# Last section of a long convolution on one Trainium2 core: inverse transform with exchanged operands, blocks turned on TensorE, additions on VectorE and GpSimd, and a new ranking of the convolution's steps

## The chip, the cores and the metric

The kernel runs on one core of one Trainium2 chip. In this text PE is TensorE, DVE is VectorE, ACT is ScalarE, POOL is GpSimd and SP the queue that starts DMA transfers. PSUM is the memory that TensorE writes. The metric is the device time of one execution in microseconds, as the median of the runs shown; smaller is better.

## What is computed

One sequence of 2,048 tokens with 512 channels goes through a state-space convolution and then through a shifting MLP, each behind a layer norm and each with a residual.

```python
def _A_ref(u, ...):                       # u: 1 x 2048 x 512, after a layer norm
    dt = jnp.exp(log_dt)
    A = -jnp.exp(log_A_real) + 1j * A_imag          # 512 x 128
    C = (C_real + 1j * C_imag) * dt[:, None]
    P = jnp.exp((A * dt[:, None])[:, :, None] * pos[None, None, :])
    K = 2.0 * jnp.einsum("dn,dnl->dl", C, P).real   # 2048 taps per channel
    y = irfft(rfft(u, 2L) * rfft(K, 2L))[..., :L]
    return y + u * D_skip
def _B_ref(x, w1, w2, w3, w4):
    h = gelu(layernorm(x) @ w1)
    hs = concat(h shifted by +1, -1, +2, -2 tokens, a quarter of the channels each) @ w2
    x1 = x + hs
    return x1 + gelu(layernorm(x1) @ w3) @ w4       # 512 -> 1792 -> 512
h  = x + _A_ref(layernorm(x), ...)
h2 = h + _B_ref(layernorm(h), ...)
```

## The kernel before, in words

**Two phases.** `conv_phase` computes the first of the last two lines, `mixer_phase` the second. The array `h` (128 partitions x 16 x 512 channels) holds the sequence in fp32: token groups q = 0 to 3 are four slices of four. The mixer starts with group 3: its normalised values are turned by PE (tiles xt), split into a high and a low part (xt30h, xt30l and so on: cast on ACT, difference on DVE), and multiplied by w1 (tiles l).

**The convolution as matmuls.** Channels are worked in four sections s of 128. The transform of length 4,096 is factored into 32 by 64 points, so each transform is two stages of small matmuls with tables: `fas` and `tbs` forward, `ms` and `fis` back. For each of eight frequency groups e, `product` (919) makes the second forward stage (matmuls of at with tbs) and multiplies spectrum and taps on DVE, or on POOL where a table says so; the results lie in u, thp, ini. `stage_b_inv` (974) then does the first inverse stage: `ms` is the stationary operand (64 x 128), the products move (128 columns), and an eviction ("ibv") writes 512 columns into at, in the order channel, k, pair. `turn_inv` (996) turns a quarter of a section with one stream transpose on DVE, in blocks of 32 by 32. `stage_a_inv` (1001) does the last inverse stage with `fis` and adds h, either with an identity matmul into the same bank and a copy by ACT, or with an addition on DVE.

**The last section.** Its last stage is `last_a_inv` (1024): four stream transposes; four identity matmuls that bring h into four banks; 64 matmuls with fis of 128 columns each, group 3 first; the statistics of group 3 straight from PSUM (DVE bn_stats); and four copies by ACT into h. After it come nodes for the norm of group 3 (1236 to 1240). The mixer's `norm1(3)` (1332) scales group 3 on DVE into the tile xq0, in a pool of its own (1253), and `turn1` (1344) has PE turn it into the four tiles xt3_0 to xt3_3. Two of these lie in the memory of banks 2 and 3 of the convolution.

**What sets the order.** In the convolution nothing is written in the order in which it runs. Each step is a node of `Plan` (153) with an engine, a cost, what it reads and writes, and a need for PSUM banks. `order` (194) fills each engine's queue step by step: among the steps that could start within 0.05 us of the first, the one with the lowest number in the table `RANK` is taken. A second table, `SHARE` (23), says which evictions go to DVE, which sums and products go to POOL, and where `pads` (759) puts two fillers. A filler (`busy`, 774) is an identity matmul of 128 columns whose result nobody reads; `order` adds more of them where its model of PE has a gap. The mixer's steps are issued in the order of the code. All instructions but a few are recorded at one line, 140, that of the helper that passes them on; names of tiles tell them apart.

## Time and profile before

| what | value |
|---|---|
| median of 3 runs | 677.06 us (676.99 to 678.91) |
| profiled execution | 676.15 us |
| its span | 673.9 us |
| its mean granted TensorE clock | 0.992 |
| PE busy | 641.1 us |
| DVE busy | 575.4 us |
| ACT busy | 403.9 us |
| POOL busy | 398.8 us |

The span runs from the first to the last instruction of the profiled execution, and 2.25 us of its time lie outside. Times in the timeline are from the span's start. A row of the timeline has the start, the length, engine, line, operation, destination and sources, and in brackets the idle time ahead of it with what ended it. An fp32 matmul leaves two records, a transpose on PE one, so "x16" of matmuls are eight of them. The chain of waits is followed back from the last instruction: each row is a stretch of the chain on one engine. The granted clock (PEclk) is shown as a share of full speed. "bank" is a PSUM bank of the convolution.

### The profile page before, as it was taken

What the parts mean: (1) busy time and instruction counts of PE and PEld (TensorE: products, weight loads), DVE (VectorE), ACT (ScalarE), POOL (GpSimd) and SP (SyncE); (2) the same over time, 40 slices, a digit from 0 to 9 for tenths busy, and PEclk for the clock granted to TensorE, in tenths of its full rate; (3) what the DMA queues carried; (4) which work ended last, traced back from release to release, by engine and by line L of the source; (5) the groups of instructions that cost most, each with busy time, mean ns of one, the idle gap of its engine ahead of it and who ended that gap; (6) DMA issues with size and microseconds to landing.
All of it is one profiled execution on the core that took longest, in us unless ns stands there. A gap on an engine that the chain in (4) does not pass through costs nothing.

```text
span 673.9 us, 17729 instructions
## 1 busy us (share of the span) xinstructions
PE 641.1 (95%) x7226; PEld 508.9 (76%) x7226; DVE 575.4 (85%) x991; ACT 403.9 (60%) x700; POOL 398.8 (59%) x411
## 2 busy tenths in 40 slices
PE   2959999999999999999999999999999999999997
PEld 2956657772777585768888888888888889999985
DVE  5999999999899999889978799866688678888896
ACT  7998879888798883246534455544465344435430
POOL 1959799899788798502676219355611644456340
PEclk9989999999899999999999999999999999999999
DMA  8944632000301233020262524455654355434104
GB/s 207 291 132 123 207 120 45 18 3 2 82 3 50 61 102 95 2 63 4 61 202 56 164 79 160 153 184 166 212 190 141 96 169 188 126 112 140 32 0 126
DMA packets 51957, 73.58 MB, mean 109 GB/s; under 512 B 7332, under 2 KB 26788, under 8 KB 51876
## 3 DMA queue, kind: packets, MB, share of 16 engines
q1 hardware_dynamic: 50212, 69.82, 34.0%
q10 hardware_dynamic: 1152, 1.57, 1.0%
q0 software_dynamic: 512, 1.05, 0.7%
q8 instruction: 57, 0.93, 0.6%
q14 instruction: 24, 0.20, 0.1%
HBM read 44.90 MB, written 21.23 MB: 98 GB/s over the span
## 4 chain that ended last, share of the span: by engine, by line
PE 70%; DVE 13%; ACT 7%; issue 3%; POOL 3%; DMA 3%; SPq 1%; DVEq 0%; ACTq 0%; POOLq 0%
PE l L140 20%; PE bank L140 14%; PE acc L140 7%; ACT pt L140 4%; DVE at L140 4%; PE l3e L140 3%; PE l3a L140 3%; PE l3d L140 3%; PE l3g L140 3%; PE l3f L140 3%; PE l3b L140 3%; PE l3c L140 3%; PE res L140 2%; DVE cs L140 2%; DMA h<-in_A_u_dram 2%
## 5 line engine op out<-in xcount | busy, mean ns | idle before, releaser
L140 POOL TENSOR_TENSOR pt<-p,s 128x512 int32<-128x512 int32 x64 | 70.9, 1120 | 6.7 <-DVE sn L140 6.0
L140 ACT ACTIVATE pt<-pt 128x1056 f32<-128x1056 int32 x64 | 69.8, 1097 | 7.6 <-DVE cs L140 4.6
L140 PE MATMUL bank<-at,tbs 128*64 128x128 f32 (+1 forms) x768 | 65.1, 314 | 2.6 <-ACT kt L140 0.9
L140 PEld LDWEIGHTS bank<-at,tbs 128*64 128x64 f32 x768 | 45.3, 135 | 18.7 <-DVE at L140 2.5
L140 PE MATMUL bank<-u,ms 64*128 64x128 f32 x736 | 47.6, 279 | 0.6 <-DVE u L140 0.4
L140 PEld LDWEIGHTS bank<-ident 128*128 128x128 f32 x310 | 37.7, 198 | 13.1 <-issue 5.2
L140 PEld LDWEIGHTS bank<-u,ms 64*128 64x128 f32 x736 | 43.0, 188 | 5.8 <-issue 2.2
L140 DVE TENSOR_TENSOR cs<-pt,amx 128x512 f32<-128x512 f32 x64 | 41.6, 679 | 2.1 <-ACT pt L140 1.5
L140 PE MATMUL bank<-ident 128*128 128x128 f32 x310 | 41.7, 288 | 0.8 <-DVE at L140 0.7
L140 POOL TENSOR_TENSOR cs<-pt,amp 128x512 f32<-128x512 f32 x26 | 32.6, 1255 | 9.4 <-ACT pt L140 5.4
L140 ACT ACTIVATE pt<-pt,halfpi 128x1056 f32<-128x1056 f32 x32 | 38.0, 1186 | 0.1
L140 POOL TENSOR_TENSOR sn<-pt,amp 128x512 f32<-128x512 f32 x28 | 34.0, 1217 | 3.8 <-issue 2.0
L140 ACT COPY at<-bank 128x512 f32<-128x512 f32 x37 | 23.1, 627 | 21.5 <-PE bank L140 21.4
L140 PE MATMUL bank<-cs 128*32 128x64 f32 x1024 | 32.4, 224 | 2.4 <-DVE cs L140 1.3
L140 DVE STREAM_TRANSPOSE at<-bank 128x512 f32<-128x512 f32 (+1 forms) x36 | 33.2, 948 | 1.1 <-PE bank L140 1.0
L140 PEld LDWEIGHTS bank<-cs 128*32 128x32 f32 x1024 | 23.8, 110 | 13.4 <-issue 4.2
L140 PE MATMUL bank<-sn 128*32 128x64 f32 x1024 | 31.9, 221 | 0.3 <-issue 0.2
L140 DVE TENSOR_TENSOR u<-xs,bank 128x1024 f32<-128x1024 f32 x23 | 27.9, 1216 | 3.4 <-ACT xs L140 3.0
L140 PE MATMUL bank<-h,fas 32*32 32x512 f32 x256 | 23.1, 752 | 6.8 <-ACT h L140 5.8
L140 DVE TENSOR_TENSOR amx<-E,amx 128x512 f32<-128x512 f32 (+1 forms) x32 | 26.4, 825 | 3.2 <-ACT amx L140 3.0
L140 POOL TENSOR_TENSOR cs0w<-raw,cs0w 128x512 fp32r<-128x512 f32 x5 | 6.5, 1299 | 36.5 <-ACT cs0w L140 36.3
L140 POOL TENSOR_TENSOR amp<-E,ec 128x512 f32<-128x512 f32 x23 | 24.6, 1074 | 4.1 <-DVE E L140 2.7
(1278 smaller groups left out, 2156.2 us busy)
## 6 DMA issues: line engine op xcount, KB each, us to landing
raw<-in_B_w_dram SPq DMA_DIRECT2D x28, 256.0 KB, 2.9
xq<-xq SPq DMA_DIRECT2D x72, 64.0 KB, 2.0
h<-in_A_u_dram SPq DMA_DIRECT2D x32, 128.0 KB, 4.1
h<-in_A_u_dram SPq DMA_DIRECT2D x16, 256.0 KB, 4.2
kept<-ptw SPq DMA_DIRECT2D x8, 512.0 KB, 4.4
ms<-in_mm_dram SPq DMA_DIRECT2D x4, 768.0 KB, 6.6
ptw<-kept SPq DMA_DIRECT2D x6, 512.0 KB, 6.0
out_dram<-h SPq DMA_DIRECT2D x48, 64.0 KB, 1.7
```

The lines of the kernel that those rows point to most:

```text
L140: ins = f(*args, **kw)
```

## The change

It has four parts.

1. **First inverse stage of the last section** (`PET = (3,)`): the products become the stationary operand and `ms` moves, 128 columns, read so that neighbours are 32 elements apart. The result has channels as partitions, and its eviction writes 512 single elements a partition in an order (x r e a b) that suits a plain 128 by 128 transpose.
2. **Turning on PE**: `turn_pe` transposes four 128 by 128 blocks into a bank, and an eviction of 512 columns ("tev", on ACT but for one on DVE) brings them back to at. The four stream transposes on DVE go.
3. **Last stage** (`last_a_back` in place of `last_a_inv`): 16 matmuls with fis of 512 contiguous columns. Only group 3 gets h by an identity matmul. For groups 0 and 2 DVE adds the bank to h; for group 1 ACT copies the bank to the memory of ms, and POOL adds that to h. The scaling of group 3, four DVE instructions, becomes a step of the plan and writes into the tile `uu`, which the convolution's buffers u0 and u1 are now parts of and which also serves as the mixer's xq0.
4. **Tables**: `RANK` and `SHARE` are new throughout, so the steps of all sections are ordered and shared out anew.

```diff
-SHARE = {'amy': [0, 1, 2, 3, 5, 6, 7, ...
+SHARE = {'tev': [(3, 7)], 'amy': [0, 1, 2, 3, 5, 6, 7, ...
...
+PET = (3,)
+TAIL = ('dve', 'pool', 'dve')
...
-    uu = [tile(f"u{i}", [128, 8 * W]) for i in range(2)]
+    cst["uu"] = tp.tile([128, 16 * W], F32, tag="uu", name="uu")
+    cst["home"] = lambda name: tp.tile([128, 16 * W], F32R, tag="uu", name=name)
+    uu = [cst["uu"][:, i * 8 * W : i * 8 * W + 8 * W] for i in range(2)]
...
+                        if s in PET:
+                            pe.matmul(plan.view(p)[:, par, pair * 128 : pair * 128 + 128], q[f, t, pair, :],
+                                      ms[f, m, e * 2 + pair, :].rearrange("p (h r i) -> p i h r", h=2, r=2),
+                                      start=(i == 0), stop=(i == len(terms) - 1))
+                            continue
                         pe.matmul(plan.view(p)[:, par, pair * w_ : pair * w_ + w_], ms[f, m, e * 2 + pair, :], q[f, t, pair, :],
                                   start=(i == 0), stop=(i == len(terms) - 1))
...
+        if s in PET:
+            dst = at[:, 0].rearrange("p (x e r a b) -> p e a b x r" if len(PET) == NS else "p (x r e a b) -> p e a b x r", e=8, r=2, a=2, b=2)[:, e]
+            src = lambda: plan.view(p)[:, :, 0:256].rearrange("p a (b x r) -> p a b x r", b=2, r=2)
...
+    def turn_pe(s, n, g, gk):
+        def tr():
+            for m in range(4):
+                i = n * 4 + m
+                pe.transpose(plan.view(p)[:, m * 128 : m * 128 + 128], at[:, 0, i * 128 : i * 128 + 128], ident)
+        p = add("PE", 0.43, tr, dense=0.0, r=[("a0", e, n) for e in RE], bank=1, w=gk)
+        evac("tev", (s, n), 512, 0.48, g, lambda: plan.view(p)[:, 0:512], w=gk, frees=p)
...
+    def last_a_back(s):
+        g = at[:, 1].rearrange("p (q i n) -> p q i n", q=4, i=2)
...
+        add("ACT", 1.5, lambda: act.activation(tiny, halfpi, AF.Sqrt), r=[("a1", q, j) for q in quads(s) for j in range(2)])
+        for q in (3, 0, 1, 2):
+            for i in range(2):
+                turn_pe(s, i * 4 + q, g[:, q, i], [("g", q, i), ("a1", q, i)])
+            if q == 3:
+                def keep():
+                    pe.matmul(plan.view(ps[3]), ident, hold(3), start=True, stop=False)
...
+            for i in range(2):
+                def mm(q=q, i=i):
+                    for c in (i, i + 2):
+                        pe.matmul(plan.view(ps[q])[quarter(c)], fis[:, c // 2, :], g[:, q, i], start=q != 3, stop=True)
...
+            if q == 3:
...
+                add("DVE", 0.85, part, r=[("bs", j) for j in range(12, 16)], w=[("hq", q), "part"])
+                add("ACT", 0.5, lambda: act.copy(hold(3), view_(3)), w=[("hq", 3), ("held", 3)], frees=ps[3])
+            elif TAIL[q] == "dve":
+                add("DVE", 0.6, lambda q=q: v.tensor_tensor(hold(q), hold(q), view_(q), ALU.add), r=HK, w=[("hq", q), ("held", q)], frees=ps[q])
+            else:
+                far_ = lambda q=q: ms[:, 0, 0:4, :]
+                add("ACT", 0.5, lambda q=q, far_=far_: act.copy(far_(), view_(q)), w=[("hq", q), ("held", q)], frees=ps[q])
+                add("POOL", 1.35, lambda q=q, far_=far_: gp.tensor_tensor(hold(q), hold(q), far_(), ALU.add), r=HK + [("held", q), "scaled"])
...
-            last_a_inv(s)
+            (last_a_back if s in PET else last_a_inv)(s)
...
+    x3 = cst["x3"] = [cst["uu"][:, i * 512 : i * 512 + 512] for i in range(4)]
+    for i in range(4):
+        add("DVE", 0.46, lambda i=i: v.tensor_scalar(x3[i], h[:, 12 + i, :], cst["mv"][:, 12 + i, 0:1], cst["norm"][2][:, 1, 12 + i : 13 + i], ALU.subtract, ALU.mult),
+            r=["norm", ("held", 3)], w=[("x3", i)] + [("u", i // 2, k) for k in range(2)] + ["scaled"] * (i == 3), port=True)
...
-    XQ = [(w1p if i else w1a).tile([128, 4 * 512], F32, tag=f"xq{i}", name=f"xq{i}") for i in range(4)]
+    XQ = [w1p.tile([128, 4 * 512], F32, tag=f"xq{i}", name=f"xq{i}") if i else cst["uu"] for i in range(4)]
...
     def norm1(q):
+        if q == 3:
+            XL[3] = list(cst["x3"])
+            return
```

In PE's queue the convolution ended before with the last inverse block (ini, ms), two fillers, the identity matmuls of h, and the narrow matmuls with fis, bank by bank:

```order
L140 MATMUL bank0_94<-ini_109,ms_101 128x128 x8
L140 MATMUL bank1_95<-ident_61 128x128
L140 MATMUL bank3_97<-ident_61 128x128
L140 MATMUL bank2_96<-h_66,ident_61 128x512
L140 MATMUL bank3_97<-h_66,ident_61 128x512
L140 MATMUL bank0_94<-h_66,ident_61 128x512
L140 MATMUL bank1_95<-h_66,ident_61 128x512
L140 MATMUL bank0_94<-at_99,fis_103 32x4x32 x16
L140 MATMUL bank2_96<-at_99,fis_103 32x4x32 x8
```

In PE's queue of the changed kernel, the same place has transposes (ident, at) and quads with fis by turns, up to the first transpose xt of the mixer:

```order
L144 MATMUL bank0_94<-ms_101,ini_109 128x128 x8
L144 MATMUL bank2_96<-h_66,ident_61 128x512
L144 MATMUL bank3_97<-ident_61,at_99 128x128 x4
L144 MATMUL bank0_94<-ident_61,at_99 128x128 x4
L144 MATMUL bank1_95<-ident_61,at_99 128x128 x4
L144 MATMUL bank2_96<-at_99,fis_103 32x512 x4
L144 MATMUL bank3_97<-ident_61,at_99 128x128 x4
L144 MATMUL bank0_94<-ident_61,at_99 128x128 x4
L144 MATMUL bank1_95<-ident_61,at_99 128x128 x4
L144 MATMUL bank3_97<-at_99,fis_103 32x512 x4
L144 MATMUL bank0_94<-at_99,fis_103 32x512 x4
L144 MATMUL bank2_96<-ident_61,at_99 128x128 x4
```

One identity matmul of h is left of four, the two fillers are gone, and the matmuls with fis stand in four quads, each behind transposes whose evictions it reads. Behind the last row come four more transposes into bank 3, the last quad into bank 2, and the transposes xt.

ACT's queue at that place in the changed kernel, from the second eviction of transposes to the cast of the mixer (rb from ra is the square root of group 3's norm):

```order
L144 COPY at_99<-bank1_95 128x512
L144 COPY at_99<-bank3_97 128x512
L144 COPY at_99<-bank0_94 128x512
L144 COPY at_99<-bank1_95 128x512
L144 ACTIVATE rb_60<-ra_59 128x2x4
L144 COPY h_66<-bank2_96 128x4x128
L144 COPY ms_101<-bank3_97 128x512
L144 COPY at_99<-bank2_96 128x512
L144 COPY at_99<-bank3_97 128x512
L144 CAST xt30h_4103<-xt3_0_4089 128x512
```

And ACT's queue at the same place before, from the load of the square root's table to the casts:

```order
L140 ACT_TABLE_LOAD
L140 ACTIVATE tiny_72<-halfpi_71 128x1
L140 COPY h_66<-bank0_94 128x4x128
L140 ACTIVATE rb_60<-ra_59 128x2x4
L140 COPY h_66<-bank3_97 128x4x128
L140 COPY h_66<-bank2_96 128x4x128
L140 COPY h_66<-bank1_95 128x4x128
L140 CAST xt30h_4110<-xt3_0_4096 128x512
```

Before, only copies into h stood there, with the square root between the first two; now the square root and two copies that free banks 2 and 3 are queued behind evictions of transposes, and the table is loaded further ahead.

The other place is PE's queue near the 64 narrow matmuls with fas and kt that come ahead of a group of taps (cs). Before:

```order
L140 MATMUL bank1_95<-h_66,fas_102 32x16x16x2 x8
L140 MATMUL bank0_94<-fas_102,kt_118 64x32 x32
L140 MATMUL bank1_95<-ident_61 128x128 x2
L140 MATMUL bank1_95<-fas_102,kt_118 64x32 x32
L140 MATMUL bank2_96<-cs0_124 32x64 x4
```

And in PE's queue of the changed kernel:

```order
L144 MATMUL bank0_94<-h_66,fas_102 32x16x16x2 x8
L144 MATMUL bank1_95<-ident_61 128x128 x2
L144 MATMUL bank1_95<-fas_102,kt_118 64x32 x32
L144 MATMUL bank0_94<-ident_61 128x128 x2
L144 MATMUL bank0_94<-fas_102,kt_118 64x32 x32
L144 MATMUL bank2_96<-cs0_124 32x64 x4
```

Two more fillers stand ahead of the first 32 narrow matmuls, and the two halves have changed places.

More of the change, by code (lines that the diff above doesn't have):

```diff
@@ L125, in tables @@
             mm[f, 2, n, r], mm[f, 2, n, i] = -st, ct
+    if len(PET) == len(WID):
+        fi = fi.reshape(2, 2, 8, 4, 64).transpose(0, 2, 1, 3, 4).reshape(128, 2, 32).copy()
     return {"fa": fa, "fi": fi, "tb": tb, "mm": mm}
@@ new lines, in stage_b_inv, with stage_a_back, mm @@
+        evac("ibv", (s, e), n, 0.22 + n * 0.51e-3, dst, src, w=keys, frees=p)
+    def turn_pe(s, n, g, gk):
[5 more added lines that the diff above has]
+        evac("tev", (s, n), 512, 0.48, g, lambda: plan.view(p)[:, 0:512], w=gk, frees=p)
+    def stage_a_back(s, q):
+        hv = h[:, q * 4 : q * 4 + 4, OFF[s] : OFF[s + 1]]
+        u = uu[q % 2].rearrange("p (i n) -> p i n", i=2)
+        hadd = OFF[s] // 64 + q // 2 in SHARE["hadd"]
+        for i in range(2):
+            turn_pe(s, i * 4 + q, u[:, i], [("u", q % 2, i)])
+        def mm():
+            b = plan.view(p)
+            if hadd:
+                pe.matmul(b, ident, hv, start=True, stop=False)
+            for c in (0, 2, 1, 3):
+                pe.matmul(b[quarter(c)], fis[:, c // 2, :], u[:, c % 2], start=not hadd, stop=True)
+        p = add("PE", 2.24 if hadd else 1.12, mm, dense=0.76, r=[("u", q % 2, i) for i in range(2)] + ["fis", ("h", s, q)], bank=1)
+        if hadd:
+            add("ACT", 0.5, lambda: act.copy(hv, plan.view(p).rearrange("p (j d) -> p j d", j=4)), w=[("h", s, q)], frees=p)
+        else:
+            add("DVE", 0.6, lambda: v.tensor_tensor(hv, hv, plan.view(p).rearrange("p (j d) -> p j d", j=4), ALU.add),
+                w=[("h", s, q)], frees=p)
@@ L1252, in mixer_phase @@
     tm = pool("tm", 6)
[L1253 removed]
+    w1p = pool("wrap", 1)
     sm = pool("sm", 2)
@@ L1758, in mixer_phase @@
             keep3(s + 1)
-    XH = [(w1p if i else w1a).tile([128, 4 * 512], F32R, tag=f"xq{i}", name=f"xh{i}") for i in range(4)]
+    XH = [w1p.tile([128, 4 * 512], F32R, tag=f"xq{i}", name=f"xh{i}") if i else cst["home"]("xh0") for i in range(4)]
     spare = w1p.tile([128, 512], F32R, tag="rawa", name="spare")
```

32 lines of the change are left out of this document (22 added, 10 removed), and 106 rows, old and new, of the table RANK.

## The prediction

> **What bounds the kernel now.** I read the page first: the busy times, and the shares of the chain of waits.
>
> ```profile
> span 673.9 us, 17729 instructions
> PE 641.1 (95%) x7226; PEld 508.9 (76%) x7226; DVE 575.4 (85%) x991; ACT 403.9 (60%) x700; POOL 398.8 (59%) x411
> PE 70%; DVE 13%; ACT 7%; issue 3%; POOL 3%; DMA 3%; SPq 1%; DVEq 0%; ACTq 0%; POOLq 0%
> ```
>
> PE is busy for 95% of the span and carries 70% of the chain. So a change pays where PE waits, or by taking PE time away. The place of this change is the end of the convolution, so I went next to the chain there (start, length, engine, destination).
>
> ```profile
> 267.39 10.98 PE bank L140 x140
> ...
> 285.03 1.18 PE bank L140 x16
> 286.23 0.61 ACT at L140
> 286.87 4.72 DVE at L140 x4
> 291.63 2.82 PE bank L140 x60
> 294.47 1.14 ACT h L140 x2
> 295.65 1.47 PE xt L140 x10
> 297.22 0.59 ACT xt30h L140
> 297.86 8.75 PE l L140 x36
> ```
>
> Until 286.2 the chain is PE alone. Then it changes engines seven times before the mixer's products (l) begin at 297.86: an eviction, four stream transposes on VectorE, the last stage of the inverse on PE, copies to h, the transposes xt, the cast. The timeline has the same stretch with what each waited for.
>
> ```profile
> 286.67 3.60 PE L140 MATMUL bank<-h,ident 128*128 128x512 f32 x8
> 286.85 1.28 ACT L140 ACT_TABLE_LOAD   x1
> 291.63 3.92 PE L140 MATMUL bank<-at,fis 128*32 128x128 f32 x104 [0.17 <-DVE at L140]
> 292.18 0.89 DVE L140 BATCH_NORM_STATS2 bs<-bank 128x6 f32<-128x128 f32 x4 [0.60 <-PE bank L140]
> 293.71 0.21 ACT L140 ACTIVATE rb<-ra 128x8 f32<-128x8 f32 x1
> 294.80 1.93 DVE L140 TENSOR_SCALAR xq<-h,mvh,rr 128x512 f32<-128x512 f32 x4
> 300.63 0.19 PEld L140 LDWEIGHTS l<-xt33l,cs0w 128*128 128x128 f32 x1 [0.34 <-DVE xt33l L140]
> ```
>
> From the last inverse product (286.2) to l (297.86) lie 11.6 us, in which PE does useful work but never all the time. The last row is PE's last wait in the first group of l: it loses 0.34 to VectorE's xt33l, so what reaches the end is what this point moves by.
>
> **The tail, step by step.** The four transposes on VectorE (4.72) and the 64 narrow matmuls go. In their place come 32 transposes on PE, eight evictions of 512 columns, and 16 matmuls of 512 columns; three of four matmuls that carry h through PSUM go (0.90 each, from the 3.60), and two additions on VectorE and one on GpSimd take their work. Prices come from these rows:
>
> ```profile
> 267.24 0.68 DVE L140 TENSOR_TENSOR h<-h,bank 128x512 f32<-128x512 f32 x1
> 267.39 1.29 PE L140 MATMUL bank<-u,fis 128*32 128x512 f32 x8
> 284.85 0.69 DVE L140 COPY at<-bank 128x512 f32<-128x512 f32 x1
> 306.44 1.91 PE L140 MATMUL xt<-ident,xq 128*128 128x128 f32 x16
> ```
>
> Four transposes cost 0.48 (a quarter of 1.91), an eviction 0.6 on ScalarE and 0.69 on VectorE, an addition out of PSUM 0.68. Four matmuls of 512 columns into the four column groups are one quad. Before, a quad reads pairs of elements and takes 1.29; a plain 512-column matmul takes 0.90. The new quads read contiguous columns, so each lies between 0.90 and 1.29, and I expect the lower half.
>
> Walk from 286.2. The eviction ends at 286.9. PE transposes group 3 and the first half of the next until 288.4; the evictions are done by 288.7; the quad of group 3 ends near 289.9, and the statistics start about 290.05, 2.1 earlier than 292.18. The square root now stands behind five evictions on ScalarE and runs near 292.0, while its input would be ready at 291.5. So the four scalings start 1.8 earlier than 294.80, at 293.0, and end at 295.0. If that were what decides, 1.8 would be won.
>
> It isn't, I think. Groups 1, 0 and 2 still go through PE, ScalarE and PE again. ScalarE's evictions end near 292.4 (six of 0.6 with PE's gaps between). Then come in its queue the square root 0.21, the copy of group 3 (0.6) that frees the bank for the last group's first four transposes, and the copy of group 1 (0.6) that frees the bank for its second four. These end near 294.4; eviction 0.6 and a hand-over take it to 295.0; the last quad ends between 295.7 and 296.5. VectorE's addition (0.69) gives 296.5 to 297.2. The first xt transpose writes the memory that this bank held, so it waits for that addition. Ten transposes at 0.12 are 1.2: 297.7 to 298.4, then the cast 0.59 and l at 298.4 to 299.1, 0.6 to 1.3 later than 297.86. Part of this is absorbed by the wait of 0.34 on xt33l, so 0.4 to 1.1 remain. With quads in their lower half I take **+0.5**. GpSimd's addition for group 1 and the load of the square root's table (1.28, now under matmuls) delay nothing: nobody but the later normalisation reads that part of h.
>
> **The operand exchange.** Eight blocks (one for each e) of 64 records swap stationary and moving operand. The nearest rows are these:
>
> ```profile
> 277.25 1.10 PE L140 MATMUL bank<-at,tbs 128*64 128x128 f32 x16
> ...
> 285.03 1.16 PE L140 MATMUL bank<-ini,ms 64*128 64x128 f32 x16 [0.23 <-DVE ini L140]
> ```
>
> Today's block streams contiguous columns in 1.16; the block before it reads pairs, 8 bytes at a time, in 1.10. Pairs cost nothing over contiguous reading. After the change each block streams ms element by element, 128 bytes apart, which no row of this kernel does. By both rows the price is zero and no gain is in it, for records and columns stay the same. The upper bound is the only ratio in the trace that reading could explain, the quad's 1.29 over 0.90, 1.43 times: 0.50 a block, 4.0 in all, in full on the chain, since PE is unbroken from 267.39. I take zero, the nearer rows. [...]
>
> The evictions of these blocks write single elements too. They keep their length of 512 columns, and lie beside PE's work, except the last, which is in the walk.
>
> **The new ranking.** The order of PE's groups before the tail is nearly unchanged. What I could price is one place, after the taps' small matmuls (columns of the windows: PE, PEld, DVE, ACT, POOL busy, PEclk).
>
> ```profile
> 168.69:172.10 3.41, 3.01 (x156) 2.74 (x155) 3.37 (x5) 3.18 (x7) 1.88 (x2) 1.00 0.80 179
> 172.10:175.51 3.41, 3.41 (x65) 2.28 (x56) 2.23 (x5) 2.99 (x5) 2.68 (x3) 0.50 0.73 135
> ```
>
> ```profile
> 170.04 17.39 PE bank L140 x372
> ```
>
> ```profile
> 171.74 0.32 PE L140 MATMUL bank<-cs 128*32 128x64 f32 x8
> ...
> 173.33 5.16 PE L140 MATMUL bank<-at,tbs 128*64 128x256 f32 x32
> 178.42 0.32 PE L140 MATMUL bank<-cs 128*32 128x64 f32 x8
> ...
> 179.45 2.06 PE L140 MATMUL bank<-u,ms 64*128 64x128 f32 x32
> 181.43 1.95 PE L140 MATMUL bank<-at,tbs 128*64 128x256 f32 x16
> 286.12 0.71 PE L140 MATMUL bank<-ident 128*128 128x128 f32 x4
> ```
>
> For 3.41 us the granted clock is 0.50. A tap group takes 1.59 there (171.74 to 173.33) and 1.03 at full clock (178.42 to 179.45): 0.56 lost. The 32 tbs records take 5.16 where two times 16 take 3.90: 1.26 lost. That is 1.8, on an unbroken PE chain. The stretch before it holds the 64 fas,kt matmuls of 32 columns; there the changed order runs two fillers (identity matmuls) more. Two fillers cost 0.55 or less (286.12 until 286.67); I reckon 0.4 as the others there overlap. If they keep the clock up, the gain is 1.8 less 0.4, **1.4**; if not, the loss is 0.4. I take the gain at about two to one. Elsewhere four fillers after the first tap go, and two sums go from GpSimd to VectorE, beside PE's work. Covers that could fail there are bounded below.
>
> **The sum.** +0.5 − 1.4 + 0 = −0.9. The profiled run took 676.15, 2.25 of it outside its span, and lies 0.9 under the median of 677.06; a difference carries over, so 677.06 − 0.9 = **676.2**.
>
> **The rivals.** *The clock stays low at 172* (0.18): tail +0.5, no gain, so 677.6. Two fillers are little against 64 narrow matmuls.
>
> *Single-element reading costs* (0.20): the exchange makes each of the eight blocks longer by up to 0.50. From the forecast it turns into slower once a block loses 0.36 (2.9 over eight), from the rival above once it loses 0.19. At the bound it gives 676.2 + 4.0 = 680.2. For it: no row shows such a read to be free. [...]
>
> *The tail loses the clock* (0.07): four stretches of mere transposes stand where broad matmuls stood. These rows are the test:
>
> ```profile
> 294.98:298.39 3.41, 3.21 (x34) 2.29 (x27) 3.41 (x10) 2.38 (x6) 0.00 (x0) 1.00 0.00 0
> 298.39:301.80 3.41, 3.41 (x15) 2.48 (x15) 3.41 (x7) 2.37 (x4) 0.00 (x0) 1.00 0.00 0
> ```
>
> The first holds the 16 transposes of xt and the next still has clock 1.00. If a window went to half clock all the same, half of 3.41 is lost, 1.7: 677.9, or 679.3 without the gain at 172. [...] The two windows speak against it here, which is why the chance is small.
>
> *More comes from the order than I priced* (0.20): the four fillers gone (0.27 each by the row above where each is seen in full, half of that where they overlap: 0.5 to 1.1), the whole 1.8, a tail at zero because the scalings are early, and up to the idle time of PE that a better order could close:
>
> ```profile
> 160.00:200.00 40.00, 39.40 (x831) 25.88 (x832) 35.54 (x52) 33.51 (x60) 33.73 (x31) 0.96 0.17 36
> ```
>
> That is 0.60 in these 40 us. Together 2.3 (0.5 and 1.8) to 3.5 (1.1, 1.8 and 0.6): 673.6 to 674.8.
>
> *The change does nothing* (0.03 left for this and a worse order): the instruction order shows all of it done, but a worse order elsewhere could cost over 2.
>
> **How the numbers follow.** Likeliest is the forecast (0.32), 676.2. About 0.3%, 2.0 us, is what a measurement of this kernel tells from no change. Faster than 675.0 is the order's case alone, 0.20. Within fall the forecast, the low clock, half of the clock loss and the cheap part of the reading rival (0.04): 0.57. Slower is the rest, 0.23. The range runs from 673.6, the low end of the order's case, to 680.2, the bound of the reads; beyond lie the reads on top of a low clock, and a worse order.
>
> **What would show it.** Exchanged blocks of 1.16 or less (right) or 1.4 and more (reads cost). A clock of 1.00 and 32 tbs records in 3.9 after the tap group near 172. Statistics near 290, the scalings near 293, yet xt not before 296.5. If xt starts ahead of 295.6, the back and forth of PE and ScalarE is cheaper than I think, and the forecast is too late.

## The result, and the profile after

| | kernel before | changed kernel |
|---|---|---|
| median | 677.13 us (6 runs, 675.31 to 678.91) | 691.70 us (6 runs, 690.99 to 698.29) |
| profiled execution, its span | 676.15, 673.9 | 691.46, 689.7 |
| mean granted clock in it | 0.992 | 0.987 |

The changed kernel is slower: the ratio is 1.0241, with a 95% interval of 1.0213 to 1.0270. (Ratios here and below come from all executions, so they differ a little from the quotient of the two medians.) The page of the changed kernel, the same three lines as before:

```profile
span 689.7 us, 17642 instructions
PE 653.3 (95%) x7180; PEld 516.9 (75%) x7180; DVE 578.2 (84%) x992; ACT 410.3 (59%) x705; POOL 398.4 (58%) x410
PE 62%; DVE 3%; ACT 2%; issue 1%; POOL 0%; ACTq 0%; DVEq 0%; POOLq 0%
```

PE is busy for 12.2 more, with 46 records fewer: the same work takes PE longer. The shares in the third line add up to 68% only, because this chain is followed back no further than 219.8; so PE's 62% is not to be compared with the 70% of before. To see where the time went, I cut both timelines at the same places. These rows of PE give the cuts, first of the kernel before, then of the changed one (first exchanged block, last one).

```profile
269.65 1.16 PE L140 MATMUL bank<-thp,ms 64*128 64x128 f32 x16
```

```profile
276.50 2.03 PE L144 MATMUL bank<-ms,thp 64*128 64x128 f32 x16
...
298.17 1.96 PE L144 MATMUL bank<-ms,ini 64*128 64x128 f32 x16
```

| stretch | before | after | difference |
|---|---|---|---|
| start to the first of the eight blocks | 269.65 | 276.50 | +6.85 |
| the eight blocks and what lies between them | 16.54 | 23.63 | +7.09 |
| end of the last block to the first product of the mixer | 11.67 | 13.90 | +2.23 |
| from there to the end | 376.06 | 375.65 | −0.41 |

**The blocks.** One exchanged block takes 1.96 to 2.03, where 1.16 stood. 0.87 times eight is 7.0, and the stretch is longer by 7.09.

**The tail.** The chain of the changed kernel there, and the timeline of the same stretch:

```profile
300.25 1.05 DVE at L144
301.44 2.92 PE bank L144 x20
304.38 0.89 DVE bs L144 x4
305.44 1.08 ACT at L144 x2
307.57 1.65 DVE uu L144
309.30 0.60 DVE h L144
...
311.26 0.60 DVE h L144
311.86 1.20 DVE bs L144 x2
313.39 0.59 ACT xt30h L144
314.03 8.54 PE l L144 x36
```

```profile
298.40 1.02 ACT L144 COPY at<-bank 128x512 f32<-128x512 f32 x1 [0.71 <-PE bank L144]
302.10 0.59 ACT L144 COPY at<-bank 128x512 f32<-128x512 f32 x1 [2.67 <-PE bank L144]
...
307.57 1.65 DVE L144 TENSOR_SCALAR uu<-h,mvh,rr 128x512 f32<-128x512 f32 x1
307.67 1.27 POOL L144 TENSOR_TENSOR h<-h,ms 128x512 f32<-128x512 f32 x1 [13.65 <-ACT ms L144]
308.91 1.54 PE L144 MATMUL bank<-at,fis 128*32 128x512 f32 x8 [0.24 <-ACT at L144]
...
311.91 1.97 PE L144 MATMUL xt<-ident,uu 128*128 128x128 f32 x16 [1.46 <-DVE h L144]
```

Two lengths are new. The eviction of an exchanged block takes 1.02 to 1.05, while the one behind a transpose takes 0.59 with as many columns. And VectorE's first scaling takes 1.65, over just the time in which GpSimd adds; the other three take 1.45 together. PE's last quad ends at 310.45, and xt waits another 1.46 for VectorE's last addition, which stands behind those scalings.

**Ahead of the blocks.** Two places of PE's timeline hold the loss. The first is at 107; before and after:

```profile
107.19 0.65 PE L140 MATMUL bank<-fas,kt 32*64 32x32 f32 x27 [0.53 <-issue]
107.77 0.94 PE L140 MATMUL bank<-ident 128*128 128x128 f32 x6
108.64 3.70 PE L140 MATMUL bank<-at,tbs 128*64 128x256 f32 x32
```

```profile
107.94 1.65 PE L144 MATMUL bank<-fas,kt 32*64 32x32 f32 x59 [1.24 <-issue]
109.52 1.65 PE L144 MATMUL bank<-ident 128*128 128x128 f32 x6
111.10 5.65 PE L144 MATMUL bank<-at,tbs 128*64 128x256 f32 x32
...
179.17 0.32 PE L144 MATMUL bank<-sn 128*32 128x64 f32 x8 [1.99 <-issue]
179.42 3.19 PE L144 MATMUL bank<-at,tbs 128*64 128x256 f32 x16
```

"issue" is a stop of PE with no releaser in the profile. In the changed kernel it is longer, and after each of the two stops all matmuls get longer. The windows show that this is the clock (PEclk is the third figure from the right), first of the kernel before, then three and one of the changed kernel:

```profile
107.10:110.50 3.40, 3.31 (x51) 2.53 (x52) 3.23 (x6) 2.82 (x7) 3.34 (x4) 1.00 0.02 5
```

```profile
104.00:107.00 3.00, 2.15 (x85) 1.18 (x69) 3.00 (x6) 2.68 (x4) 2.13 (x3) 1.00 0.40 68
107.00:110.00 3.00, 2.06 (x61) 2.00 (x62) 2.92 (x6) 1.55 (x4) 3.00 (x4) 0.72 0.02 5
110.00:113.00 3.00, 3.00 (x16) 2.00 (x17) 0.92 (x3) 2.97 (x6) 2.93 (x4) 0.50 0.00 0
```

```profile
180.20:181.90 1.70, 1.70 (x10) 0.95 (x8) 0.63 (x1) 1.54 (x3) 1.27 (x2) 0.50 0.04 10
```

So the low clock at 172 did not go; it came at 180 instead, behind a stop of 1.99, and another one came at 107. The first place puts the changed kernel 4.4 behind (the tbs matmuls end at 116.75 where they ended at 112.34), the second another 1.9 (the next tap group starts at 184.72, after 178.42: 6.3). Executions of one kernel differ in this: of the six of the changed kernel the fastest has a mean clock of 0.987 (690.99) and the slowest 0.979 (698.29).

### The profile page after: what moved, and what is told of

It is laid out like the page before. It is cut to its first block, busy times and chain, and to the rows that moved or that the text cites. A ratio compares the mean times of both kernels' runs of the same rounds, so it can differ in the third digit from the quotient of the medians.

```text
span 689.7 us, 17642 instructions
## 1 busy us (share of the span) xinstructions
PE 653.3 (95%) x7180; PEld 516.9 (75%) x7180; DVE 578.2 (84%) x992; ACT 410.3 (59%) x705; POOL 398.4 (58%) x410
## 3 DMA queue, kind: packets, MB, share of 16 engines
q0 software_dynamic: 512, 1.05, 0.7%
## 4 chain that ended last, share of the span: by engine, by line
PE 62%; DVE 3%; ACT 2%; issue 1%; POOL 0%; ACTq 0%; DVEq 0%; POOLq 0%
PE l L144 20%; PE bank L144 8%; PE acc L144 7%; PE l3a L144 3%; PE l3d L144 3%; PE l3g L144 3%; PE l3f L144 3%; PE l3e L144 3%; PE l3c L144 3%; PE l3b L144 3%; PE res L144 2%; DVE uu L144 1%; PE l4y L144 1%; PE l4x L144 1%; PE l4z L144 1%; PE l4w L144 1%
## 5 line engine op out<-in xcount | busy, mean ns | idle before, releaser
L144 PE MATMUL bank<-at,tbs 128*64 128x128 f32 (+1 forms) x768 | 68.0, 323 | 3.4 <-ACT at L144 1.6
L144 ACT COPY at<-bank 128x512 f32<-128x512 f32 x45 | 30.7, 692 | 32.8 <-PE bank L144 32.3
L144 PEld LDWEIGHTS bank<-ident 128*128 128x128 f32 x334 | 40.4, 198 | 9.7 <-issue 5.0
L144 PE MATMUL bank<-uu,ms 64*128 64x128 f32 x672 | 43.7, 279 | 1.2 <-DVE uu L144 0.5
L144 PEld LDWEIGHTS bank<-uu,ms 64*128 64x128 f32 x672 | 39.3, 188 | 6.4 <-POOL uu L144 1.9
L144 PE MATMUL bank<-ident 128*128 128x128 f32 x334 | 43.9, 287 | 0.0
L144 DVE TENSOR_TENSOR uu<-xs,bank 128x1024 f32<-128x1024 f32 x23 | 27.8, 1214 | 1.4 <-ACT xs L144 0.7
L144 PE MATMUL bank<-h,fas 32*32 32x512 f32 x256 | 21.6, 755 | 5.6 <-ACT h L144 5.0
L144 PEld LDWEIGHTS bank<-sn 128*32 128x32 f32 x1024 | 24.2, 111 | 3.4 <-issue 2.2
```

Source lines behind the costliest of these rows:

```text
L144: ins = f(*args, **kw)
```

## The experiments

My theory after the result had three parts: single-element reading makes the blocks longer (7.0), the new order makes the clock fall (6.9), and the tail loses 2.2 by the long eviction and the hold-up on VectorE. The rivals were that the exchange itself costs, and that the falls of the clock come from elsewhere. Sixteen kernels followed. Each was compared with the kernel before on the same chip. Each run's median is of 4 to 12 executions, which differ by up to 7 us where the clock falls in some of them; steps of 1 or 2 us between two medians are therefore read from the traces as well.

| run | median | kernel before | ratio, 95% interval |
|---|---|---|---|
| e1 old ranks | 686.84 | 676.12 | 1.0159 (1.0129 to 1.0188) |
| e2 new ranks alone | 688.43 | 676.12 | 1.0165 (1.0126 to 1.0205) |
| e3 ms contiguous | 687.93 | 676.12 | 1.0147 (1.0097 to 1.0198) |
| e4 both | 681.81 | 676.12 | 1.0076 (1.0053 to 1.0100) |
| e5 fillers put back | 682.59 | 676.84 | 1.0081 (1.0055 to 1.0108) |
| e6 before without fillers | 676.87 | 676.84 | 1.0000 (0.9984 to 1.0016) |
| e7 eviction in 16 bytes | 680.13 | 676.84 | 1.0051 (1.0035 to 1.0068) |
| e8 additions on VectorE | 684.97 | 676.84 | 1.0109 (1.0078 to 1.0140) |
| e9 GpSimd later | 679.23 | 677.47 | 1.0025 (1.0005 to 1.0046) |
| e10 before, two fillers | 676.12 | 677.47 | 0.9981 (0.9963 to 1.0000) |
| e11 five fillers | 682.52 | 677.47 | 1.0067 (1.0035 to 1.0098) |
| e12 all so far | 679.74 | 677.47 | 1.0034 (1.0018 to 1.0051) |
| e13 load later | 678.51 | 677.02 | 1.0018 (0.9990 to 1.0046) |
| e14 before, load later | 676.67 | 677.02 | 0.9984 (0.9957 to 1.0010) |
| e15 all, load later | 677.15 | 677.02 | 0.9998 (0.9973 to 1.0023) |
| e16 repaired ranks alone | 678.00 | 676.53 | 1.0019 (0.9998 to 1.0040) |

**e1 and e2: the ranking apart from the last section.** The plan numbers its steps in the order of the code, and the first 1,217 are the same in both kernels. So ranks and shares can be exchanged up to there: e1 has the old ranks for these steps and the old SHARE but for 'tev', e2 the new ones.

```diff
-SHARE = {'tev': [(3, 7)], 'amy': [0, 1, 2, 3, 5, 6, 7, ...
+SHARE = {'tev': [(3, 7)], 'amy': [0, 1, 2, 3, 5, 6, 7, ...
...
 RANK = (
-    87, 80, 105, 106, 104, 110, 111, 109, 112, 121, 118, 114, 131, 127, 137, 142, 119, 129, 130, 113, 139, 120, 135, 136,
+    142, 141, 181, 176, 177, 196, 201, 193, 200, 192, 187, 198, 206, 229, 205, 231, 218, 217, 194, 197, 221, 219, 223, 225,
...
```

> The changed kernel with the old tables: every step up to the last section has the rank and the engine it had before, and only the last section's own steps keep their new ranks. Theory: of the 15.3 us, 6.9 are lost by the new ranking ahead of the first exchanged block (276.50 against 269.65 in the two profiles), most of it in a stretch of low clock at 107 to 115. Then this run takes 691.7 - 6.9 = 684.8, its clock stays at 1.00 from 104 to 118, and the first exchanged block starts near 269.7. Rival: the loss there is no matter of the order (it comes with the shared tile for u0 and u1, or of itself); then it stays near 691.7, with the low clock.

> The kernel before with the new tables for every step up to the last section; operands, stream transposes and last stage are the old ones. If the ranking alone loses the 6.9 us, it takes 677.1 + 6.9 = 684.0 and shows the low clock at 107 to 115. If the loss needs the new last section or the shared tile, it stays at 677, within 1.5.

e1 took 686.84: 4.9 less than the changed kernel by the medians, 3.9 if each is taken against its own kernel before (10.7 and 14.6), not 6.9. Its profile has clock 1.00 from 104 to 118 and the first exchanged block at 272.2. It has a fall of the clock at 221 instead. e2 took 688.43: the new ranks alone cost the old kernel 11 to 12, more than in the changed kernel. Its profile has half clock at 107, 178, 226 to 237 and 270 to 278. So the ranking is a cause by itself, and its price changes with how many of these places are hit. It also changes from one execution to the next: with the old tables for these steps the first exchanged block comes between 268.73 (e7) and 274.06 (e9), and with the new ones at 276.50 in the changed kernel and 280.33 in e3, which have one and the same order on PE. The price is known to a few us only.

**e3: ms read contiguously.** The order of the columns is put right by the eviction.

```diff
-                                      ms[f, m, e * 2 + pair, :].rearrange("p (h r i) -> p i h r", h=2, r=2),
+                                      ms[f, m, e * 2 + pair, :],
...
-            dst = at[:, 0].rearrange("p (x e r a b) -> p e a b x r" if len(PET) == NS else "p (x r e a b) -> p e a b x r", e=8, r=2, a=2, b=2)[:, e]
-            src = lambda: plan.view(p)[:, :, 0:256].rearrange("p a (b x r) -> p a b x r", b=2, r=2)
+            dst = at[:, 0].rearrange("p (i h e a b) -> p e a b h i", h=4, e=8, a=2, b=2)[:, e]
+            src = lambda: plan.view(p)[:, :, 0:256].rearrange("p a (b h i) -> p a b h i", b=2, h=4)
```

> The changed kernel, with ms read in its own order, contiguously, as the moving operand; the order is put right by the eviction, which writes single elements as before, only in another sequence. Theory: the exchanged block takes 2.03 instead of 1.16 because ms is read in single elements 128 bytes apart. Then the block goes to about 1.16, and 691.7 - 8 x 0.87 = 684.7. Rival: the exchange itself costs it (the products as stationary operand, or the load of weights); then blocks stay near 2.03 and the time near 691.7.

A group of these matmuls (busy, mean ns) in the changed kernel; the same group in e3, and e3's first block:

```profile
L144 PE MATMUL bank<-ms,uu 64*128 64x128 f32 x64 | 7.9, 403 | 0.5 <-ACT at L144 0.4
```

```profile
L144 PE MATMUL bank<-ms,uu 64*128 64x128 f32 x64 | 4.4, 281 | 0.3 <-ACT at L144 0.2
```

```profile
280.33 1.16 PE L144 MATMUL bank<-ms,thp 64*128 64x128 f32 x16
```

The mean of one falls from 403 to 281 ns, and the block to 1.16, just as the block before the change. The eight blocks with what lies between them go from 23.63 to 17.02: 6.6 of the 7.1 are the reading, and the exchange of the operands is free. The 0.5 that is left goes with the evictions (e12 below, with both edits, has 16.53, as before the change). The time fell by 3.8 and not 7.0, since e3's profiled execution loses more to the clock (mean 0.979, with a long fall at 224 to 235): its first block starts at 280.33, where the changed kernel's starts at 276.50, though PE's order is the same. Its four executions take 681.3 to 688.6. The same edit on the old tables (e1 to e4, one chip) is worth 5.0 by the medians and 7.2 in this stretch (24.94 to 17.78).

**e4: both.** The edits of e1 and e3.

> Both edits: old tables ahead of the last section, and ms read contiguously. If the two losses add, 691.7 - 6.9 - 7.0 = 677.8, about the time of the kernel before; what is left above 677.1 is the tail (2.2 longer in the profile from the last inverse product to the mixer's first product). If they are one and the same loss, it takes about 684.

681.81, 4.0 over what the sum gave. In the profiles e4 is 6.4 behind the kernel before: 2.1 in the tail, 1.2 among the blocks, 1.4 ahead of them (a fall of the clock at 221) and 1.6 in the mixer. Of the 1.2, some 0.7 are work that stands there with the old tables, not waits, and 0.5 are waits for the long evictions (e7 takes them off). The work is this row:

```profile
286.65 1.12 PE L144 MATMUL bank<-h,ident 128*128 128x512 f32 x2
```

**e5 and e6: the fillers.** The new table has no fillers at four places at which the old one has two each. e5 is e3 with them put back; e6 is the kernel before with m = 0 at the same four places.

```diff
         n = 2 if key in SHARE["pad"] else 0
-        return n, cost + 0.23 * n, ...
+        m = 2 if key in (('a', 0, 0, 0), ('a', 2, 0, 1), ('t', 3, 0, 0), ('t', 3, 1, 0)) else n
+        return m, cost + 0.23 * n, ...
```

> The changed kernel with ms read contiguously (687.9 in the run before, its profile with half clock at 108, 176, 224 to 235 and 268), plus two fillers at each of the four places where the old table had them and the new one has none: ahead of the narrow matmuls of the taps' spectra in sections 0, 2 and 3. The order of all else is unchanged. Theory: taking these eight fillers away is what lets the clock fall at 107, 224 and 268. Then the stretches at these three places go, the mean clock rises from 0.98 to 0.99, and the time falls by 5 to 8, to 680 to 683. Rival: the clock falls there because of the new order (waits and gaps on PE), and eight fillers of about 0.2 change little: 687 to 690.

> The kernel before, with its order, but without the fillers at these four places (eight identity matmuls less, nothing else). If the fillers hold the clock, half-clock stretches appear near 107, 220 and 265, the mean clock falls from 0.99 to 0.98, and it takes 680 to 686 where the kernel before takes 676 to 677. If the order is the cause, it takes 675 to 677, a little less for the fillers' own time.

Both outcomes together are the finding. In the new order eight fillers are worth about 5: 687.93 to 682.59 by the medians, 4.5 by the ratios (1.0147 to 1.0081). The intervals of the two ratios overlap a little, but the mean clock over all executions points the same way, 0.982 in e3 and 0.989 in e5, and the falls at 107, 224 and 268 are gone from the profile. In the old order the same fillers are worth nothing (676.87 against 676.84; mean clock 0.991, and 0.993 before). The new order leaves stretches that need them, and the new table took them away there. What stayed in e5 was the stop at 173 and a fall of the clock behind it.

**e7: the eviction in groups of four.** On e4.

```diff
-            dst = at[:, 0].rearrange("p (i h e a b) -> p e a b h i", h=4, e=8, a=2, b=2)[:, e]
-            src = lambda: plan.view(p)[:, :, 0:256].rearrange("p a (b h i) -> p a b h i", b=2, h=4)
+            dst = at[:, 0].rearrange("p (i h e a b) -> p e i h a b", h=4, e=8, a=2, b=2)[:, e]
+            src = lambda: plan.view(p)[:, :, 0:256].rearrange("p a (b h i) -> p i h a b", b=2, h=4)
```

> Old tables and contiguous ms (681.8 before), and the eviction of the exchanged blocks writes groups of four neighbours (16 bytes) and reads PSUM in single elements, where it wrote single elements 512 bytes apart. Theory: the scattered writing is what makes this eviction 1.03 long instead of 0.61; then it falls to 0.6 to 0.7, PE's waits among the last blocks shrink (2.3 to 2.1 a block), and the time falls by 1 to 1.5 to about 680.5. Rival: any single-element pattern on one side costs the same; then the eviction stays near 1.0 and the time near 681.8.

The last eviction of e7's timeline:

```profile
286.05 0.58 ACT L144 COPY at<-bank 128x512 f32<-128x512 f32 x1 [2.40 <-PE bank L144]
```

From 1.02 to 0.58. The blocks' stretch is shorter by 0.50 (17.78 to 17.28) and the tail by 0.42 (13.81 to 13.39): 0.9 in all by the traces. By the medians it is 1.7 (681.81 to 680.13), with intervals that overlap. Writing single elements far apart was the price: 512 bytes in e3 and e4, 128 and 256 in the changed kernel, with the same 1.02 to 1.05. Reading PSUM in single elements shows none: 0.58 here, against 0.61 for the last eviction of the kernel before.

**e8: all additions on VectorE.** On e4.

```diff
-TAIL = ('dve', 'pool', 'dve')
+TAIL = ('dve', 'dve', 'dve')
```

> Old tables and contiguous ms (681.8 before), and group 1 of the last stage is added to h by VectorE straight from PSUM like groups 0 and 2: no copy to ms on ScalarE, no addition on GpSimd. Theory: GpSimd's addition holds up VectorE's first scaling (1.65 in place of 0.48, over the time of GpSimd's 1.27), and with it VectorE's last addition, on which xt waits. Then the scalings take 0.48 each, xt starts 0.5 to 1.0 earlier after the last inverse product, and the time is about 681. Rival: the third addition costs VectorE what it wins (0.67), and nothing changes by over 0.3.

A miss: 684.97, 3.2 slower than e4 by the medians (the intervals overlap); the tail takes 17.15 where e4's takes 13.81. The scalings do take 1.91 for four, but they now stand ahead of the addition that frees the bank of a filler before the last quad, and PE waits for it, and later once more ahead of xt; in between the clock falls. Two rows of PE, and two windows:

```profile
301.37 0.49 PE L144 MATMUL bank<-ident 128*128 128x128 f32 x2 [1.19 <-DVE h L144]
...
303.70 3.46 PE L144 MATMUL xt<-ident,uu 128*128 128x128 f32 x16 [0.86 <-DVE h L144]
```

```profile
302.00:304.00 2.00, 1.14 (x6) 0.30 (x3) 1.00 (x2) 0.00 (x0) 0.00 (x0) 0.85 0.00 0
304.00:306.00 2.00, 2.00 (x11) 2.00 (x10) 1.18 (x4) 0.00 (x0) 0.00 (x0) 0.50 0.04 8
```

**e9: GpSimd behind the scalings.** On e7.

```diff
-                add("POOL", 1.35, lambda q=q, far_=far_: gp.tensor_tensor(hold(q), hold(q), far_(), ALU.add), r=HK + [("held", q), "scaled"])
+                cst["add1"] = lambda q=q, far_=far_: gp.tensor_tensor(hold(q), hold(q), far_(), ALU.add)
...
+    def add1():
+        gp.tensor_copy(tiny, x3[3][:, 0:1])
+        cst["add1"]()
...
+    add("POOL", 1.45, add1, r=[("x3", i) for i in range(4)] + [("held", 1)] + [("h", 3, r) for r in R4])
```

> The run with old tables, contiguous ms and 16-byte eviction (680.1 before), with GpSimd's addition of group 1 put behind VectorE's four scalings: a copy of one element of the last scaling stands ahead of it on GpSimd, so that it starts when they are done. Theory: while GpSimd adds (1.27), VectorE's scaling stands still (1.65 instead of 0.48), and VectorE's last addition, which xt waits for, comes 0.7 late. Then four scalings take 1.9 together, xt starts 10.6 after the last exchanged block ends instead of 11.3, and the time falls by 0.7, to 679.4. Rival: the 1.65 has another cause (a wait that the profile counts as busy); then the first scaling stays long and the time at 680.1.

```profile
298.27 1.92 DVE L144 TENSOR_SCALAR uu<-h,mvh,rr 128x512 f32<-128x512 f32 x4
...
302.01 1.96 PE L144 MATMUL xt<-ident,uu 128*128 128x128 f32 x16 [0.86 <-DVE h L144]
```

Four scalings take 1.92, and xt starts 10.66 after the last block instead of 11.26. The whole tail goes from 13.39 to 12.78, by 0.6; the time falls by 0.9 by the medians (the ratio from 1.0051 to 1.0025, with intervals that overlap).

**e10: the step at 172 in the old order.** On the kernel before.

```diff
+        m = 2 if key in (('a', 1, 1, 1),) else n
```

> The kernel before with two fillers more, ahead of the other half of the narrow matmuls before the low clock at 172; nothing else. It is the step of the prediction that forecast a gain of 1.4 from these two fillers. By the prediction: clock 1.00 at 172 to 176 and 1.4 less. By what the runs have shown since (the changed kernel has the two fillers and its clock falls at 178 all the same): the low clock stays in most executions, and the time stays within 0.5 of the kernel before.

The prediction's step holds here: the window that had clock 0.50 has 1.00, the mean clock over all executions is 0.9935 against 0.9916, and the time is 1.35 less (676.12 against 677.47, just at the edge of what the interval can tell).

```profile
172.10:175.51 3.41, 3.41 (x134) 2.71 (x128) 2.90 (x6) 3.37 (x5) 1.74 (x2) 1.00 0.98 189
```

**e11 and e12: more fillers at 172, and all of it.** e11 is e5 with five fillers instead of two ahead of both halves; e12 adds the edits of e7 and e9.

```diff
+        m = 5 if key in (('a', 1, 1, 0), ('a', 1, 1, 1)) else m
```

> The run with the fillers put back (682.6 before; its profile has PE idle for 2.06 with no releaser in the middle of a tap group at 173, and half clock from 174 to 181), with five fillers instead of two ahead of each half of the narrow matmuls there, 1.5 more work for PE. Theory: the instructions run out where 256 narrow matmuls follow one another, PE stands still for 2, and by that the clock falls and costs some 3.5 more; with more time for fewer instructions ahead of it the stop shrinks below 0.5 and the clock holds: 682.6 + 1.5 - 2 - 3 = 679. Rival: the stop does not come from the number of instructions, and stays: 684.

> The changed kernel with everything that helped by then or should: contiguous ms, 16-byte eviction, fillers put back and five at 172, GpSimd's addition behind the scalings; the new order. From the run with the fillers put back (682.6): 1.7 off for the eviction, 0.7 for the addition, 3.5 for the clock at 174: 676.7, no better than the kernel before (676.8). What stays against it is the tail, about 1 longer than before. Rival: the gains don't add, because the clock falls elsewhere in turn: 679 to 682.

e11's profile kept its clock at 174 (a fall came at 263 instead), but the stop is still 2.13, and the time 682.52:

```profile
176.24 0.32 PE L144 MATMUL bank<-sn 128*32 128x64 f32 x8 [2.13 <-issue]
```

So more time ahead of the string of narrow matmuls did not shorten the stop here; e12's profile, with the same five fillers, has 0.79 at the same place. e12 took 679.74, 3.0 more than I had reckoned.

**e13 to e15: the load of h.** What the stops among the narrow matmuls at 173 to 179 have in common is that SP's four loads of the next residual (1 MB) run at the time. In these runs the loads for sections 0 and 1 have to wait until the narrow matmuls are through. e13 is e5 with this edit and e14 is e10 with it; e15 is e12 with it, and with two fillers where e12 has five.

```diff
             for c in R4:
-                add("SP", 0.4, dma(h[quarter(c), :, OFF[s] : OFF[s + 1]], xv[c][:, :, OFF[s] : OFF[s + 1]]),
+                def go(c=c):
+                    if s not in FAR:
+                        dma(h[32 * c : 32 * c + 1, 0, OFF[s] : OFF[s] + 2], view(s, 1)[0:1, 16:18, 0, 0])()
+                    dma(h[quarter(c), :, OFF[s] : OFF[s + 1]], xv[c][:, :, OFF[s] : OFF[s + 1]])()
+
+                add("SP", 0.4, go,
+                    r=[("a1", HB[s] // 32 + q, j) for q in R4 for j in range(2)] if s not in FAR else [],
                     w=[("h", s, q) for q in range(WID[s] // 32)])
```

> The run with contiguous ms and the fillers put back (682.6 before; PE stands still for 2.06 at 173 and half clock follows from 174 to 182), with the four loads of h for sections 0 and 1 made to start only when the narrow matmuls of the taps' spectra are through: each is preceded by a transfer of two elements that reads what those matmuls left and writes where the load then writes. The order on PE, ACT, DVE and GpSimd is the same. Theory: the stop is PE's supply of instructions, which comes late while 1 MB of data moves; without the burst the stops at 107 and 173 go, the clock holds there, and the time falls by 3 to 5, to 678 to 679.5. Rival: the stop comes from the string of narrow matmuls alone, whatever the transfers do: it stays at 1 to 2, and the time at 682 to 683 (or more, if the late load makes someone wait).

> The kernel before with the two fillers of the run e10 (676.1, against 677.5 of the kernel before) and the same delay of the loads. The old order has a stop of 0.5 to 1.1 at 107 and a fall of the clock at 172 in some executions. If the burst is the cause of both, it takes 674.5 to 675.5; if not, 676 to 677.

> The changed kernel with contiguous ms, 16-byte eviction, GpSimd's addition behind the scalings, the fillers put back (two at each place) and the delay of the loads. By the sum from the run e12 (679.7, with five fillers at two places): 1.5 less for these fillers and 1 less for the stop, so 677.2; by the rival of the run e13, 680 to 681.

The windows of e5, where the stop is (the last two figures are the DMA share and GB/s), with the row behind the stop, and the same of e13:

```profile
172.00:174.00 2.00, 1.09 (x66) 0.89 (x58) 1.40 (x3) 2.00 (x3) 0.52 (x1) 1.00 1.22 225
174.00:176.00 2.00, 0.85 (x14) 0.68 (x16) 0.00 (x0) 0.18 (x2) 0.59 (x2) 0.59 0.29 51
```

```profile
175.15 0.32 PE L144 MATMUL bank<-cs 128*32 128x64 f32 x2 [2.06 <-issue]
```

```profile
172.00:174.00 2.00, 2.00 (x103) 1.84 (x96) 2.00 (x5) 1.94 (x5) 1.54 (x2) 1.00 0.04 8
174.00:176.00 2.00, 1.68 (x86) 1.38 (x80) 1.63 (x3) 2.00 (x3) 0.29 (x1) 1.00 0.00 0
```

```profile
175.50 0.26 PE L144 MATMUL bank<-cs 128*32 128x64 f32 x3 [0.32 <-issue]
```

With the load out of the way the stop is 0.32 instead of 2.06, the clock holds here, and the time falls by 4.1, to 678.51. So in this order moving the load takes most of the stop away. The load alone does not make one: the kernel before and e10 run the same load beside their narrow matmuls (a DMA share of 0.98 in e10's window above) and PE does not stop. Nor does every stop need a load. At 107, e14 has this row with a DMA share of 0.03 and less around it, a fall of the clock behind it, and no gain over e10:

```profile
107.55 0.65 PE L140 MATMUL bank<-fas,kt 32*64 32x32 f32 x27 [0.81 <-issue]
```

e15, the change with all repairs, equals the kernel before: 677.15 against 677.02.

**What the stops wait for.** The page lists two DMA queues as "instruction". In the changed kernel q8, the larger one, carries 56 packets in 0.92 MB, about 16 KB each:

```profile
q8 instruction: 56, 0.92, 0.5%
```

The trace has the start and end of each packet. Between 60 and 300 us the 18 profiles have 51 stops put down to "issue" that are longer than 0.25 us. All 51 end 1.2 to 1.6 us after such a packet has ended; a moment taken at random lies that close behind a packet in 6.5% of the time. The stop of 1.24 at 107 ends 1.44 after one, the stop of e14 there 1.50 after one, so this holds with no load too. In e5 a packet runs from 172.49 to 173.75 and the stop ends at 175.15. In e13 the packet comes 1.6 earlier in PE's work (it starts 0.15 ahead of the second group of narrow fas,kt matmuls, and 1.44 behind it in e5), and the stop is 1.74 shorter. From this I read that PE waits for its instructions in these stops. That is an estimate read from times, and no run moved the packets alone; why a packet comes late beside the load in this order, and at 107 without a load, stays open.

**e16: the mended ranks in the old kernel.** New tables ahead of the last section on the kernel before, with the edits of e5 and e13.

> The kernel before (old operands, stream transposes on VectorE, old last stage) with the new tables ahead of the last section, the fillers put back and the delay of the loads. From the run e15 (677.15, against 677.02 of the kernel before) less the longer tail (1.3): 675.8, if the new order is as good as the old one once mended. Rival: the new order is worse by itself and e15 owes its time to something in the new last section: then 677 to 679.

A miss, 678.00, in the range that the expectation gave to its rival. But the profile does not show the rival's worse order ahead of the mixer; the convolution does end earlier: l begins at 296.41, 1.45 ahead of the kernel before. But from there to the end it takes 377.9 instead of 376.1. PE has two waits in the mixer that the kernel before has not:

```profile
326.54 0.73 PE L140 MATMUL l<-xt10h,sn0w 128*128 128x512 f32 x2 [0.58 <-ACT xt10h L140]
```

```profile
401.22 0.50 PE L140 MATMUL l3e<-t100h,cs1w 128*128 128x512 f32 x1 [0.67 <-DVE u L140]
```

They are 1.25 of the 1.8. The second does not come from the earlier start: e1, e4, e7, e8 and e9 have it too, with 0.52 to 0.80, and their mixers start later than that of the kernel before; the changed kernel does not have it. What makes these waits is open. And they are a part of the answer only, for this profiled execution (676.36) is the fastest of the twelve, 1.6 under their median.

## Why the prediction was wrong

**The exchanged blocks: the failed step is "I take zero, the nearer rows".** Forecast 0, bound 4.0, measured 7.1 for the stretch, of which e3 shows 6.6 to be the reading. The mechanism stood among the rivals. Two things were mis-sized. Pairs and contiguous reading cost the same (1.10 and 1.16), and from that I went on to single elements, where no row was. And the bound was no bound: 1.43 came from another pattern, the pairs of a quad's 512 columns, and a block grew by 1.75 (2.03 over 1.16). That the mean of one record grew by about as much as 1.43 (from 279 to 403 ns, 1.44 times) is chance. What the traces show is a block of 1.10 with pairs, 1.16 with contiguous reading and 2.03 with single elements 128 bytes apart; why single elements take longer is not shown.

**The evictions: the failed step is "They keep their length of 512 columns, and lie beside PE's work".** The columns stayed, the time did not: measured 1.03 instead of 0.61, and back to 0.58 in e7. By e7's traces it is worth 0.9, of which 0.5 lie among the blocks and 0.4 in the tail; the medians would have 1.7.

**The ranking: the failed step is "The order of PE's groups before the tail is nearly unchanged. What I could price is one place".** Forecast −1.4, measured +6.85 in the profile, +3.9 to +4.9 by e1. The one place was priced rightly for the old order, as e10 shows (1.35). In the new order PE stopped there for 2 in the string of narrow matmuls, and the clock fell behind it; e13 shows 4.1 for what went with this. And "four fillers after the first tap go" was booked as work saved, in the rival on the order; the table takes eight at four places. e5 shows that taking them away was a cost of about 5, e6 that this could not be read from the old order. I had looked at what the order does to waits that the trace shows, and not at what the fillers do for the clock (a mean of 0.982 without them in e3, 0.989 with them in e5).

Two smaller points of the same part: the rival of the low clock at 172 is priced at 677.6, with no gain, although by its own reckoning the two fillers then lose 0.4, which makes 678.0. And "a worse order elsewhere could cost over 2" named what came, but had next to no chance.

**The tail: a size was off.** Forecast +0.5 from a walk of 0.6 to 1.3 at l; measured +2.23. Of that, the long eviction is 0.4 (from the last block's end to l, 288.87 to 302.68 in e4 and 286.00 to 299.39 in e7: 13.81 and 13.39) and GpSimd's addition 0.6 (e9). With both repaired, e12 and e15 have 12.95 against 11.67: 1.3 is left, the upper end of the walk's 0.6 to 1.3, not its lower half. The order of events in the walk held, and so did the 0.34 on xt33l: that wait is gone, and the stretch from l to the end is 0.41 shorter, so that +1.8 reach the end where +0.5 was forecast. "GpSimd's addition … delay nothing" was the wrong sentence. The traces show VectorE held up: 1.65 for a scaling of 0.48 beside GpSimd's addition, and 1.92 for all four in e9, where the addition comes after them. The addition itself takes 1.27 in the changed kernel and 1.26 in e9, so it is not slowed. By what means it holds VectorE up is not shown.

**The rival on the clock in the tail** did not come in the changed kernel (clock 1.00 there). It came in e8, in a stretch that holds transposes and a wait of PE of 1.2 us ahead of them; which of the two does it is not shown.

**The whole.** 691.7 goes to 687.9 by contiguous ms, 682.6 by the fillers, 678.5 by moving the load, 677.15 by the eviction and GpSimd's place: 14.5 of the 14.6 (medians, with the kernel before between 676.1 and 677.5 on these chips). By the ratios to the kernel before it is 1.0241, 1.0147, 1.0081, 1.0018 and 0.9998. The last step is within the intervals; the traces price it at 1.4 (0.5 among the blocks, 0.9 in the tail), as the medians do. What remains open: what makes PE stop at 107 and at 173 to 179 (if it is the instruction packets, why they come late there), and what makes the waits in the mixer.

## What to carry to other kernels

A pattern that the trace of before doesn't show has no price there. If the change reads or writes single elements where pairs or rows stood, a ratio from another pattern is no bound on it (1.43 was taken, 1.75 came): leave the upper end open, or measure the pattern alone first. A filler that looks idle can be what holds the clock (eight of them were worth about 5 in e5), so its removal is costed with the clock lost and not with its own time gained; that holds for a new order even when it doesn't for the old one. And a schedule made against a model should be checked against the trace: here for stops of PE in strings of narrow matmuls (2.06 in e5), and for an engine that holds another up (a VectorE scaling of 1.65 instead of 0.48 beside GpSimd's addition).

## What the runs showed of the hardware

- A moving operand read in single fp32 elements 128 bytes apart made a block of 16 records 2.03 instead of 1.16; pairs of 8 bytes cost nothing (1.10 for a block of as many).
- An eviction that writes single elements 512 bytes apart took 1.02, one with 128 and 256 bytes between them 1.02 to 1.05; in groups of 16 bytes 0.58, though it then read PSUM in single elements.
- PE stood still for 2.06 in the middle of narrow matmuls while a load held the DMA engines at a share of 1.22, and for 0.32 with the load moved away; with five fillers in place of two ahead of it the stop was 2.13 in e11 and 0.79 in e12. In the kernel before (shares of 1.09 to 1.23) and in e10 (0.98) the same load stopped nothing.
- All 51 stops of PE without a releaser over 0.25 us, between 60 and 300 us of the 18 profiles, end 1.2 to 1.6 after a packet of about 16 KB on q8, the larger of the two DMA queues that the page lists as "instruction".
- Eight identity matmuls of 128 columns whose results nobody uses were worth about 5 in one order of the same work (mean clock 0.982 without, 0.989 with them) and nothing in another (0.991 and 0.993).
- A VectorE scaling of 0.48 took 1.65 beside a GpSimd addition of 1.27; with the addition behind the scalings (1.26), four of them took 1.92.
